# Sixteen row loads from SyncE's queue to ScalarE's and a new order of the words after chunk 2's casts, in a chunked retention that feeds a GELU MLP

## The chip, the core and the metric

The kernel runs on one core of a Trainium2 chip. The metric is device time in microseconds of one launch. Five compute engines take part: TensorE (PE; its weight loads are shown as PEld), VectorE (DVE), ScalarE (ACT), GpSimd (POOL) and SyncE (SP), which here only issues DMAs. DMAs issued by SyncE, ScalarE and GpSimd stand in three queues (SPq, ACTq, POOLq). Each engine runs its instructions in the order of the program; between engines there are semaphores.

## The reference, cut to what matters

```python
B, H, S, D = 4, 8, 768, 64
gamma = 1.0 - 2.0 ** (-5.0 - np.arange(H))
state = np.zeros((B, H, D, D))
for t in range(S):
    state = gamma * state + einsum('bhd,bhe->bhde', k[:, :, t], v[:, :, t])
    y[:, :, t] = (1 / sqrt(D)) * einsum('bhd,bhde->bhe', q[:, :, t], state)
x = y.transpose(0, 2, 1, 3).reshape(B * S, H * D)      # 3072 x 512
h = x @ w_in                                           # 512 x 2048
g = 0.5 * h * (1.0 + np.tanh(c * (h + 0.044715 * h**3)))
out = g @ w_out                                        # 2048 x 512
```

Everything is float32 outside. Inside, the products take float16 operands and add up in float32.

## The kernel before

**Tiling.** The 768 tokens are cut into six chunks c = 0 to 5 of 128, with four batches b each; a chunk is thus 512 rows of the MLP. For each chunk and batch the rows of q, k and v are loaded as float32 tiles of 128 tokens by 512 (`L`, L308, tile r, 256 KB each, thirteen buffers), and cast or scaled to float16 (`PREP`: q and k give the tile qk, v from chunk 2 on is scaled by a constant). q and k are transposed: in chunks 0 and 1 by TensorE with a copy (`T`, `ET`), in chunks 2 to 5 by a transposing DMA on SyncE's queue (`DT`, L345). `A` makes the scores of a chunk on TensorE, `EA` scales them with the mask on VectorE, `YP` and `YI` make the output of a chunk from the state and from the scores, `EP` writes it to the tile x on VectorE with a decay. `SS` and `ES` (L430, four VectorE instructions) bring the state to the next chunk.

**The MLP.** Both products go by a Winograd form: seven products of half size in place of eight. It wants sums of blocks: of w_in (`WI`), of w_out (`WO`), of x (`SX`, tile sx, four a chunk) and of g (`SG`, tile sg, four for each chunk and each j). These sums are additions of two float16 tiles in SBUF of 128x512 and can stand on VectorE or on GpSimd. j = 0 to 3 numbers the quarters of the 2048 hidden columns. `M1:c,j,n` is product n of the first matrix product: four matmuls of 128x256 into one of three PSUM banks X, Y, Z of its (c, j). `CP` copies a bank to a tile h, `D1` adds a bank to h on VectorE (L216), `G` takes the GELU on ScalarE (L442) and writes g. `M2:c,n,a,f` is a part, again of four matmuls, of product n of the second matrix product; `CO`, `D2` and `ST` copy, add and store its result. Part of chunk 0 is computed without that form (`HB`, `GB`, `O0`, `EO`, `ST0`). A product M1:c,j,1 needs the x of its chunk's batches 0 and 1, thus `EP:c,0,0` and `EP:c,0,1`; its bank must have been read by the last user, which for M1:2,3,1 in the new text is EP:2,1,1 and for M1:3,0,1 is EP:3,0,0. Where a product adds to a bank that a copy or an addition still reads, it waits too: M1:3,0,4 adds to the bank that D1:3,0,22 reads. M1:3,0,6 needs the sum SX:3,2.

**What sets the order.** The text `ORDER` (L17 to L135) holds 1125 words. Lines L656 to L661 take one word after another and emit its instructions, so each engine's and each queue's order is that of its words in this text. The letter in a word is its engine (`V` VectorE, `A` ScalarE, `P` GpSimd, `S` SyncE); the numbers behind `@` are the buffers that it takes; a buffer that comes again makes the new word wait for the last reader of the old contents. A word `L:v,4,0,S@10` loads the rows of v of chunk 4, batch 0, on SyncE's queue into buffer 10. `HOLD` is a DMA of a few bytes on SyncE's queue that reads a weight tile, so what stands behind it waits until that tile has been loaded. `LD` loads a constant, `LWI` and `LWO` (L262, L267) load the weights through GpSimd's queue.

```python
    for word in ORDER.split():
        word, _, at = word.partition("@")
        kind, _, args = word.partition(":")
        slots[:] = at.split(",") if at else []
        made[kind](*(int(x) if x.lstrip("-").isdigit() else x for x in args.split(",") if x))
```

Two lines are shared by many kinds: L216 is every two-operand elementwise instruction (`EA`, `EP`, `SX`, `SG`, `WI`, `WO`, `D1`, `D2`, scaled casts), L219 every matmul. Copies and casts are L211 on ScalarE and L213 on the others.

## Time and profile before

| what | value |
|---|---|
| time, median of 3 runs (lowest to highest) | 200.77 us (200.41 to 201.9) |
| the profiled execution's own time | 200.09 us |
| its span, first to last instruction | 198.3 us |
| TensorE busy (share of the span), matmuls | 183.0 us (92%), 2111 |
| VectorE busy, instructions | 160.0 us (81%), 294 |
| GpSimd busy, instructions | 139.1 us (70%), 143 |
| ScalarE busy, instructions | 119.3 us (60%), 219 |
| mean granted clock of TensorE | 0.98 |
| DMA moved | 34.26 MB, mean 173 GB/s |

Times in the profile are microseconds from the start of the span; durations in the groups are a mean in ns. A line of the timeline has the start, the busy time, the engine, the line, the operation and its tiles (out<-in), how many in a row (x4) and, in brackets, how long the engine stood idle before it and what ended that. A start to the next start on the same engine is a step; two instructions in a row overlap a little, so that steps are shorter than single durations. The stretches list for each engine its busy time and its instructions between two moments. The table of the slices has one digit for each fortieth of the span, the busy share in tenths. The chain that ended last is followed back from the last instruction.

### The profile page before, as it was taken

What the parts mean: (1) busy time and instruction counts of PE and PEld (TensorE: products, weight loads), DVE (VectorE), ACT (ScalarE), POOL (GpSimd) and SP (SyncE); (2) the same over time, 40 slices, a digit from 0 to 9 for tenths busy, and PEclk for the clock granted to TensorE, in tenths of its full rate; (3) what the DMA queues carried; (4) which work ended last, traced back from release to release, by engine and by line L of the source; (5) the groups of instructions that cost most, each with busy time, mean ns of one, the idle gap of its engine ahead of it and who ended that gap; (6) DMA issues with size and microseconds to landing.
All of it is one profiled execution on the core that took longest, in us unless ns stands there. A gap on an engine that the chain in (4) does not pass through costs nothing.

```text
span 198.3 us, 5294 instructions
## 1 busy us (share of the span) xinstructions
PE 183.0 (92%) x2111; PEld 149.0 (75%) x2111; DVE 160.0 (81%) x294; ACT 119.3 (60%) x219; POOL 139.1 (70%) x143
## 2 busy tenths in 40 slices
...
DVE  0888979899678999998989999998897577674630
...
GB/s 144 288 239 243 203 334 234 295 239 333 270 195 235 214 211 258 213 212 216 244 226 190 209 178 155 53 150 27 94 0 0 86 23 58 106 0 56 141 201 136
DMA packets 80540, 34.26 MB, mean 173 GB/s; under 512 B 69060, under 2 KB 78404, under 8 KB 80516
## 3 DMA queue, kind: packets, MB, share of 16 engines
...
## 4 chain that ended last, share of the span: by engine, by line
PE 65%; DMA 19%; POOL 6%; DVE 4%; issue 2%; ACT 1%; ACTq 0%; SPq 0%; POOLq 0%; DVEq 0%
PE bank L219 65%; DMA w_in<-in_moe_w_in_dram 9%; DMA r<-in_q_dram 6%; DMA qkT<-qk 2%; DVE g L216 2%; DMA r<-in_v_dram 2%; POOL sx L216 2%; POOL t_out L216 1%; POOL qk L216 1%; POOL v L216 1%; DVE h L216 1%; DVE w_out L216 1%; POOL g L216 1%; POOL w_in L262 0%; POOL qk L213 0%
## 5 line engine op out<-in xcount | busy, mean ns | idle before, releaser
L219 PEld LDWEIGHTS <-g 128*128 128x128 f16 x624 | 60.4, 98 | 11.8 <-PE bank L338 0.3
L216 POOL TENSOR_TENSOR g<-g 128x512 f16<-128x512 f16 x46 | 54.5, 1204 | 17.9 <-DVE g L216 7.2
L219 PE MATMUL bank<-w_out,g 128*128 128x256 f16 (+1 forms) x384 | 60.4, 290 | 0.2 <-DMA w_out<-in_moe_w_out_dram 0.2
L216 DVE TENSOR_TENSOR h<-bank,h 128x512 f32<-128x512 f32 x69 | 46.0, 682 | 8.8 <-PE bank L219 4.4
L442 ACT ACTIVATE g<-h 128x512 f16<-128x512 f32 x69 | 42.7, 634 | 15.4 <-DVE h L216 15.0
L219 PEld LDWEIGHTS <-w_in 128*128 128x128 f16 x432 | 39.2, 98 | 6.2 <-issue 0.8
L211 ACT COPY h<-bank 128x512 f32<-128x512 f32 x57 | 32.7, 588 | 13.0 <-PE bank L219 12.6
L219 PEld LDWEIGHTS <-t_in 128*128 128x128 f16 x276 | 26.4, 98 | 9.9 <-issue 4.3
L219 PE MATMUL bank<-t_out,g 128*128 128x256 f16 x240 | 33.4, 273 | 0.0
L216 DVE TENSOR_TENSOR a<-bank,mask 128x512 f16<-128x512 f32 x48 | 30.0, 680 | 3.5 <-PE bank L219 3.4
L219 PE MATMUL bank<-x,w_in 128*128 128x256 f16 (+1 forms) x248 | 29.7, 259 | 0.4 <-DMA w_in<-in_moe_w_in_dram 0.2
L219 PE MATMUL bank<-sx,t_in 128*128 128x256 f16 x184 | 26.5, 273 | 2.3 <-ACT g L442 1.2
L219 PE MATMUL bank<-sx,w_in 128*128 128x256 f16 x184 | 26.7, 273 | 0.0
L216 DVE TENSOR_TENSOR g<-g 128x512 f16<-128x512 f16 x34 | 22.1, 669 | 3.1 <-ACT g L442 2.1
L442 ACT ACTIVATE g<-bank 128x512 f16<-128x512 f32 (+1 forms) x31 | 16.5, 549 | 8.4 <-PE bank L219 5.8
L211 ACT COPY o<-bank 128x512 f32<-128x512 f32 (+1 forms) x19 | 9.7, 516 | 18.2 <-PE bank L219 18.2
L216 POOL TENSOR_TENSOR v<-r,cst 128x512 f16<-128x512 f32 x16 | 16.9, 1061 | 4.0 <-DMA r<-in_v_dram 4.0
L216 DVE TENSOR_TENSOR o<-bank,o 128x512 f32<-128x512 f32 (+1 forms) x18 | 10.6, 595 | 8.9 <-PE bank L219 8.7
L211 ACT CAST qk<-r 128x512 f16<-128x512 f32 x20 | 12.1, 620 | 6.2 <-PE bank L219 2.2
L219 PE MATMUL bank<-x,t_in 128*128 128x256 f16 x92 | 13.8, 273 | 1.9 <-DVE h L216 1.9
L216 DVE TENSOR_TENSOR qk<-r,cst 128x512 f16<-128x512 f32 x13 | 9.2, 744 | 6.5 <-DMA cst<-rr_cst 4.1
L211 ACT COPY qkT<-bank 128x1024 f16<-128x1024 f16 x7 | 6.9, 1013 | 8.0 <-PE bank L338 8.0
...
## 6 DMA issues: line engine op xcount, KB each, us to landing
r<-in_v_dram SPq DMA_DIRECT2D x15, 256.0 KB, 4.8
r<-in_q_dram SPq DMA_DIRECT2D x15, 256.0 KB, 4.2
r<-in_k_dram SPq DMA_DIRECT2D x14, 256.0 KB, 4.6
out_dram<-o ACTq DMA_DIRECT2D x11, 256.0 KB, 3.8
r<-in_v_dram POOLq DMA_DIRECT2D x9, 256.0 KB, 8.3
out_dram<-o SPq DMA_DIRECT2D x9, 256.0 KB, 2.3
w_in<-in_moe_w_in_dram POOLq DMA_DIRECT2D x8, 256.0 KB, 9.6
r<-in_k_dram POOLq DMA_DIRECT2D x8, 256.0 KB, 8.6
```

The costliest lines, as they stand in the source:

```text
L211: nc.scalar.copy(out=out, in_=in_)
L216: EN[e].tensor_tensor(out=out, in0=in0, in1=in1, op=op)
L219: nc.tensor.matmul(out=out, lhsT=lhsT, rhs=rhs, start=start, stop=stop, skip_group_check=True)
L442: nc.scalar.activation(out=out, in_=in_, func=AF.Gelu_apprx_tanh, scale=1.0)
```

## The change

Both texts hold 1125 words and the same products, sums, copies and stores; what differs is order, engine and buffer. TensorE's first 79 words, VectorE's first 76, ScalarE's first 65, GpSimd's first 40 and the first 10 words of SyncE's queue have the same engine and order as before, with some buffers exchanged; this is about the first 52 us. Behind that point:

- Sixteen loads of rows go from SyncE's queue to ScalarE's. In ScalarE's order they are k,3,2 k,3,3 q,3,0 v,3,3 k,3,0 q,3,3 v,4,3 q,4,3 v,4,0 k,4,0 q,5,0 v,5,1 k,5,2 v,5,0 k,5,0 k,5,3. SyncE keeps 28 of its 44; GpSimd's 23 loads stay with it.
- 28 sums (three `SX`, the rest `SG`, `WO` and `WI`) go from GpSimd to VectorE, 21 go the other way. 17 copies (`CP`, `CO`) go from ScalarE to VectorE, 13 the other way. Eight casts go from ScalarE to GpSimd, six the other way. Six stores go from SyncE's queue to ScalarE's, four the other way. VectorE has 274 words where it had 263, ScalarE 248 for 236, GpSimd 130 for 135, SyncE 65 for 83.
- The words of all engines stand in a new order.

The stretch from chunk 2's transposes to D1:3,0,22, and the last words, in both texts:

```diff
--- before.py
+++ after.py
 ORDER = """
...
-DT:2,3@1 CP:1,1,22,V@0 WO:3,1,P D1:1,0,11 PREP:k,2,2,A@3 L:v,2,1,S@6 M1:1,0,6 O0:2,0@6 CP:1,3,12,V@3
-PREP:q,2,2,P PREP:v,2,2,P@0 M1:1,0,5@4 PREP:k,2,0,A@4 G:1,0,11@18 M1:1,3,7 M1:1,3,3 PREP:q,2,1,A CP:1,0,12,A@1
-WI:1,2,V O0:2,1 PREP:q,2,0,P DT:2,1@2 DT:2,2@3 D1:1,3,22 LD:S D1:1,3,12 M1:1,1,6 EO:1,A@1 DT:2,0@0 HOLD:1,3
-M1:1,1,3 L:v,3,3,S@1 WO:3,2,P G:1,3,22@19 CP:1,1,12,A@2 M1:1,0,7 WI:1,4,P G:1,3,12@20 M1:1,3,4 D1:1,1,12
-G:1,3,21@21 A:2,3@2,5 M1:1,1,7 M1:1,2,5@7 O0:2,2 M1:1,2,1@1 EA:2,3,1@0 CP:1,0,22,A@3 PREP:v,2,1,P@3 D1:1,0,22
-D1:1,1,22 WO:1,2,P G:1,1,12@22 G:1,1,22@23 EA:2,3,0 M1:1,0,3 L:k,3,0,S@2 M1:1,0,4 D1:1,0,12 O0:2,3
-CP:1,2,22,V@2 CP:1,2,11,A@0 L:k,3,2,S@8 L:v,3,0,S@3 G:1,0,21@24 M1:1,1,4 M1:1,2,6 L:q,3,3,S@11 A:2,1@5,2
-G:1,1,21@25 PREP:v,3,2,P@2 A:2,2@4,3 L:q,4,1,S@7 EO:2,V@2 EA:2,1,0@3 EA:2,2,1@1 G:1,0,22@26 A:2,0@0,6
-CP:1,2,12,A@3 G:1,0,12@27 PREP:v,2,0,P@1 WO:0,2,P EA:2,0,0@2 L:q,3,2,S@5 PREP:v,2,3,P@4 M1:1,2,3 O0:3,0@5
-O0:3,1 EA:2,0,1 L:q,3,0,S@4 M1:1,2,7 PREP:k,3,0,A@1 EA:2,1,1 YP:2,0@3,0 EA:2,2,0 L:k,3,3,S@0 L:k,5,1,S@6
-YP:2,1@6,2 D1:1,2,12 YI:2,0 SG:1,1,1,P@28 L:q,3,1,S@10 PREP:v,3,3,P@6 L:q,4,2,S@12 SG:1,3,1,P@29 YI:2,1 YI:2,2
-HOLD:0,0 YI:2,3 EP:2,0,1,V@0 SS:2,0@4 SS:2,3@7 D1:1,2,22 SS:2,2 EP:2,0,0,V SS:2,1 SG:1,1,2,P@30 ES:2,1,V
-PREP:k,3,2,A@4 L:k,3,1,S@9 O0:3,2 G:1,2,22@31 M1:1,2,4 M1:1,2,2@0 EP:2,1,1,V O0:3,3 M1:2,0,1@3 D1:1,2,11
-WO:0,3,P HOLD:0,3 WO:3,3,P ST0:2,S PREP:q,3,2,P L:v,3,1,S@2 PREP:q,3,3,A@0 M2:1,1,0,0@7 EP:2,1,0,V
-SG:1,1,4,V@32 M1:2,3,1@2 M2:1,2,0,0@0 EO:3,A@3 CP:2,0,11,A@1 M1:2,0,2@6 M1:2,3,2@5 SX:2,1,V@3 G:1,2,21@33
-G:1,2,12@34 M2:1,2,0,1 SG:1,0,3,V@35 G:1,2,11@36 PREP:q,3,0,A CP:2,3,11,A@2 M1:2,0,5@1 SX:2,2,V@2
-CP:2,0,22,A@3 L:k,4,0,S@1 M2:1,1,1,0 SG:1,0,1,V@37 ES:2,0,V M1:2,0,6 PREP:q,3,1,A@3 D1:2,3,11 M1:2,3,6
-SG:1,0,2,V@38 M2:1,1,1,1 SX:2,4,P@4 M2:1,5,0,0@4 CP:2,0,12,A@0 M1:2,0,3 M2:1,1,0,1 G:2,3,11@39 M2:1,2,1,0
-SX:2,3,V@0 CP:2,3,12,A@2 M2:1,5,1,0 M1:2,0,7 M1:2,3,7 L:q,5,3,S@8 SG:1,3,2,V@40 SG:1,2,1,V@0 DT:3,0@4
-D1:2,0,12 PREP:k,3,1,A SG:1,3,4,P@2 M2:1,5,0,1 SG:1,2,2,P@6 L:q,4,0,S@5 CO:1,11,A@4 D1:2,0,11 G:2,0,12@9
-D1:2,0,22 WO:2,3,P WO:1,3,V G:2,0,22@1 M1:2,3,5@5 CP:2,3,22,A@0 WO:2,4,P DT:3,2@5 M2:1,2,1,1 PREP:k,3,3,A
-M2:1,5,1,1 SG:1,0,4,V@3 PREP:q,4,2,A@2 D1:2,3,22 L:k,4,3,S@11 M1:2,1,5@1 G:2,0,11@13 L:v,4,2,S@4 M1:2,0,4
-D2:1,11, DT:3,3@6 M1:2,3,3 M1:2,3,4 DT:3,1@0 D1:2,3,12 M1:2,1,1@6 G:2,0,21@14 L:v,4,0,S@10 M1:2,1,2@0
-CP:2,1,22,V@3 CO:1,22,A@5 G:2,3,21@4 SG:1,2,4,P@5 CP:2,1,11,A@1 M2:1,6,1,0 M2:1,3,0,0 SG:1,2,3,V@7 M2:1,6,1,1
-M1:2,1,6 G:2,3,22@8 D1:2,1,11 PREP:v,3,1,P@5 G:2,3,12@11 A:3,0@5,3 A:3,2@2,0 PREP:v,3,0,P@7 L:k,4,1,S@9
-SG:2,0,3,P@12 SG:1,1,3,P@10 CP:2,1,12,A@0 M1:2,1,3 M2:1,3,0,1 M2:1,6,0,0 WO:3,4,V EA:3,2,0@2 M1:2,2,1@2
-M2:1,6,0,1 M2:1,3,1,0 M1:2,1,7 CO:1,12,A@2 M2:1,3,1,1 SG:1,3,3,P@15 EA:3,0,0@3 D1:2,1,12 EA:3,0,1 EA:3,2,1
-D1:2,1,22 A:3,3@5,1 A:3,1@3,0 M1:2,1,4 L:q,4,3,S@0 G:2,1,21@24 EA:3,3,0@1 EA:3,3,1 EA:3,1,1@0 EA:3,1,0
-L:v,5,2,S@12 CP:2,2,11,A@2 M2:1,7,1,0 M2:1,7,1,1 L:k,4,2,S@2 M2:1,7,0,0 PREP:v,4,0,P@1 D2:1,12, ST0:0,S
-YP:3,1@6,5 YP:3,0@1,0 YI:3,2 WO:0,4,P WO:1,4,P YI:3,3 SS:3,3@3 G:2,1,12@18 L:v,5,0,S@3 YI:3,0 G:2,1,22@22
-YI:3,1 EP:3,1,1,V@1 SS:3,1@4 G:2,1,11@28 EP:3,0,1,V SS:3,2 PREP:q,4,3,A@0 PREP:k,4,3,A SS:3,0 EP:3,0,0,V
-M2:1,7,0,1 D2:1,22, M1:2,2,5@5 PREP:k,4,2,P SG:2,1,1,P@37 EP:3,1,0,V M1:2,2,6 M1:2,2,2@0 M1:3,0,1@1
-CP:2,2,22,A@0 CP:2,2,12,A@3 CP:3,0,11,A@1 ES:3,1,V M2:1,4,1,0 M1:2,2,7 D1:2,2,22 M2:1,4,1,1 PREP:q,4,0,A@3
-PREP:k,4,0,P ES:3,0,V M2:1,4,0,0 PREP:v,4,2,P@4 SX:3,1,P@1 M1:2,2,3 SX:3,3,P@5 M1:3,1,1@6 D1:2,2,11
-L:q,5,1,S@10 L:q,5,0,S@0 M2:2,1,0,0@3 M1:3,0,2@4 DT:4,2@2 G:2,2,22@20 ST:1,12,S SX:3,2,P@3 M2:2,1,1,0
-M1:3,1,2@0 M2:1,4,0,1 PREP:k,5,1,P@4 PREP:q,5,1,P PREP:k,4,1,A@1 D1:3,0,11 CP:3,1,11,A@0 M2:2,2,0,0@4
-D1:2,2,12 M1:3,0,5@5 PREP:q,4,1,P G:2,2,11@0 M1:2,2,4 D1:3,1,11 CP:3,0,22,V@2 SX:3,4,V@2 SG:2,0,1,V@29
-SG:2,3,1,V@27 SG:2,3,2,P@34 M1:3,0,6 M2:2,1,0,1 G:3,0,11@33 G:2,2,12@36 SG:2,1,2,V@17 CO:1,21,A@0
-SG:2,0,2,P@25 G:2,2,21@30 SG:2,1,3,V@38 M2:2,2,0,1 M1:3,0,3 M1:3,1,6 L:v,4,3,S@11 CP:3,0,12,A@1 G:3,1,11@6
-L:k,5,0,S@2 CP:3,1,12,A@3 M1:3,1,5@0 A:4,2@7,2 SG:2,2,1,V@40 CP:3,1,22,A@0 DT:4,3@1 M2:2,2,1,0 D1:3,0,12
-EA:4,2,0@2 L:k,5,3,S@5 SG:2,0,4,P@3 M1:3,0,7 L:q,5,2,S@1 DT:4,0@3 D1:3,0,22 M2:2,2,1,1 M1:3,1,7 M2:2,1,1,1
...
-D2:5,22,0 ST:5,22,S,0 M2:5,4,1,0 D2:5,12,0 M2:5,4,0,0 ST:5,22,S,1 ST:5,12,S,0 CO:4,21,A@1 M2:5,4,1,1
-M2:5,4,0,1 M2:5,3,1,0 ST:4,21,A CO:5,21,A,1@4 M2:5,3,1,1 CO:5,21,A,0 D2:5,12,1 ST:5,21,A,0 ST:5,21,S,1
-ST:5,12,S,1
...
+DT:2,1@1 D1:1,0,22 D1:1,1,22 O0:2,3 D1:1,0,12 M1:1,2,1@0 G:1,1,12@22 DT:2,3@2 M1:1,1,4 SG:1,3,1,V@23 DT:2,2@3
+A:2,3@5,2 G:1,0,22@24 A:2,1@7,1 WO:1,2,P L:k,3,3,A@4 M1:1,0,4 CP:1,2,11,A@3 G:1,1,21@25 EA:2,3,1@0 G:1,1,22@26
+EO:2,A@2 DT:2,0@0 L:v,2,1,S@0 PREP:v,2,0,P@2 L:v,3,0,S@5 G:1,0,21@27 O0:3,0@6 LD:S M1:1,2,6 M1:1,2,5@2
+EA:2,1,0@3 A:2,2@3,4 EA:2,1,1 SG:1,3,2,V@28 SG:1,3,3,P@29 CP:1,2,12,A@2 SG:1,0,1,V@30 L:q,3,0,A@12 A:2,0@7,1
+WO:2,4,P PREP:v,3,2,P@1 CP:1,2,22,A@0 PREP:v,2,2,P@3 M1:1,2,7 EA:2,2,1@1 O0:3,1 EA:2,2,0 EA:2,0,0@2 EA:2,0,1
+WO:3,1,P M1:1,2,3 O0:3,2 L:q,3,1,S@1 EA:2,3,0 PREP:v,2,1,P@6 YP:2,0@4,3 YP:2,1@7,1 L:v,3,3,A@2 L:k,3,1,S@11
+D1:1,2,12 YI:2,0 SS:2,3@5 YI:2,2 YI:2,1 D1:1,2,22 EP:2,0,0,V@0 SG:1,0,3,P@31 SS:2,1@2 EP:2,0,1,V G:1,2,12@32
+G:1,2,22@33 SS:2,0 YI:2,3 PREP:k,3,2,A@3 SG:1,1,1,P@34 SS:2,2 L:q,3,2,S@3 O0:3,3 PREP:k,3,3,P@1 EP:2,1,1,V
+L:k,3,0,A@9 M1:1,2,2@4 M2:1,1,0,0@3 EO:3,A@3 D1:1,2,11 G:1,0,12@35 M1:2,3,1@1 L:k,5,1,S@7 EP:2,1,0,V M1:1,2,4
+L:v,3,1,S@6 CP:2,3,11,A@2 L:q,3,3,A@10 PREP:v,3,0,P@5 PREP:q,3,0,A@2 M2:1,1,1,0 ES:2,0,V L:q,4,1,S@0
+SX:2,1,V@3 WO:3,2,V M1:2,0,1@6 M2:1,5,0,0@4 ES:2,1,V PREP:q,3,1,P@4 M1:2,3,2@7 G:1,2,11@36 CP:2,0,11,A@0
+M2:1,2,0,0@2 M2:1,2,1,0 SX:2,3,P@2 SX:2,2,P@0 M2:1,1,1,1 M2:1,2,1,1 M2:1,1,0,1 L:q,4,2,S@8 SG:1,0,2,V@37
+SX:2,4,P@4 WO:1,3,V M1:2,0,6 D1:2,3,11 G:1,2,21@38 ST0:0,S M2:1,5,1,0 SG:1,0,4,P@39 M1:2,0,2@5 PREP:k,3,1,A
+CO:1,11,V@4 L:k,4,2,S@4 M1:2,3,5@7 M1:2,3,6 PREP:k,3,0,A DT:3,0@4 CP:2,0,12,V@1 M1:2,0,7 M1:2,0,5@0
+SG:1,2,1,V@40 M2:1,5,1,1 D1:2,0,11 PREP:q,3,2,A G:2,3,11@0 CP:2,3,12,A@3 SG:1,2,2,V@2 DT:3,2@5 PREP:q,3,3,A
+M2:1,2,0,1 SG:1,1,2,V@6 M1:2,3,7 DT:3,1@6 G:2,0,11@9 CP:2,0,22,A@2 CP:2,3,22,A@0 L:v,4,3,A@5 SG:1,1,3,V@1
+WO:0,3,V L:q,4,3,A@12 M2:1,5,0,1 DT:3,3@0 M1:2,1,2@5 D2:1,11, M1:2,3,3 D1:2,3,22 M1:2,1,1@2 D1:2,0,22
+M2:1,6,1,0 G:2,3,22@3 D1:2,3,12 M2:1,6,0,0 M1:2,0,3 SG:1,2,4,P@13 CP:2,1,11,A@0 L:q,4,0,S@1 SG:1,1,4,P@14
+D1:2,1,11 M1:2,0,4 CO:1,22,A@5 D1:2,0,12 M1:2,3,4 G:2,3,12@4 L:k,4,1,S@11 M1:2,1,6 G:2,0,21@5 A:3,2@7,5
+SG:1,3,4,P@21 A:3,0@0,6 G:2,3,21@7 M2:1,3,1,0 SG:1,2,3,V@8 EA:3,2,0@2 PREP:v,3,1,P@4 CP:2,1,12,A@3 M1:2,1,5@1
+M2:1,6,0,1 G:2,0,22@11 EA:3,0,1@1 M1:2,1,7 M2:1,6,1,1 L:v,4,0,A@9 EA:3,2,1 M2:1,3,0,0 EA:3,0,0 WO:1,4,P
+PREP:v,4,3,P@7 PREP:v,3,3,P@6 CP:2,1,22,A@2 WO:3,3,P G:2,1,11@12 WO:3,4,P A:3,1@7,6 D1:2,1,22 A:3,3@5,0
+EA:3,1,0@3 M1:2,1,3 M1:2,1,4 M1:2,2,1@7 M2:1,3,1,1 G:2,1,21@27 EA:3,3,0@0 EA:3,1,1 EA:3,3,1 M2:1,3,0,1
+PREP:k,5,1,P@0 L:v,4,2,S@3 YP:3,0@2,5 L:k,4,3,S@10 CO:1,12,A@0 L:q,5,1,S@6 YP:3,1@6,0 YI:3,2 D2:1,12,
+D1:2,1,12 YI:3,3 YI:3,0 YI:3,1 SS:3,0@4 SS:3,3@1 SS:3,2 CP:2,2,11,A@0 EP:3,1,0,V@1 SS:3,1 WO:2,3,P EP:3,0,0,V
+M1:2,2,6 G:2,1,22@10 L:v,5,2,S@5 EP:3,1,1,V M2:1,7,0,0 M2:1,7,1,0 M2:1,7,1,1 L:v,4,1,S@2 M1:2,2,5@6 EP:3,0,1,V
+PREP:q,4,2,P@2 M2:1,7,0,1 G:2,1,12@15 SX:3,1,V@5 CP:2,2,12,A@2 HOLD:0,0 PREP:q,4,3,A@1 M1:2,2,7 WO:0,4,V
+SG:2,3,1,P@16 G:2,0,12@18 PREP:k,4,2,P L:k,4,0,A@7 CP:2,2,22,A@3 M1:3,0,1@2 SG:2,0,1,P@30 D2:1,22, SX:3,2,P@1
+M1:3,0,2@0 ES:3,0,V M1:2,2,2@5 SG:2,3,2,V@35 CP:3,0,11,A@1 M2:1,4,1,0 ST:1,11,A D1:2,2,11 PREP:q,5,1,P
+D1:3,0,11 M1:2,2,3 M2:1,4,0,0 L:q,5,0,A@8 D1:2,2,12 M1:3,0,6 ES:3,1,V L:q,5,3,S@12 PREP:q,4,0,P@3 PREP:k,4,3,A
+M2:1,4,1,1 M2:2,1,0,0@4 M1:3,0,5@5 G:2,2,11@34 SX:3,4,P@0 M2:2,1,1,0 DT:4,2@1 CP:3,0,22,V@0 M1:3,1,1@0
+ST:1,12,A M1:3,1,2@6 PREP:k,4,0,A DT:5,1@2 G:2,2,12@17 SX:3,3,P@3 PREP:v,4,0,P@2 D1:2,2,22 M2:2,1,0,1
+G:3,0,11@25 CP:3,1,11,A@2 M2:1,4,0,1 M2:2,2,0,0@1 CO:1,21,V@4 SG:2,3,4,V@23 M2:2,1,1,1 SG:2,0,2,V@40
+G:2,2,22@37 PREP:q,4,1,A@4 SG:2,1,1,P@32 CP:3,0,12,A@1 D1:3,1,11 DT:4,0@3 L:v,5,1,A@4 M1:3,1,6 PREP:k,4,1,A
+M1:2,2,4 M1:3,0,3 M1:3,0,7 CP:3,1,12,V@3 G:2,2,21@6 SG:2,1,2,P@22 DT:4,3@4 D1:3,0,22 SG:2,1,3,P@19 M2:2,2,0,1
...
+M2:5,3,0,1 CO:4,21,V@0 M2:5,4,1,0 D2:5,12,0 M2:5,4,1,1 ST:3,21,A D2:5,11,1 M2:5,7,0,1 CO:5,21,V,1@3 ST:4,21,A
+M2:5,3,1,0 M2:5,3,1,1 D2:5,22,0 ST:4,12,S M2:5,4,0,0 D2:5,12,1 ST:5,21,A,1 ST:5,11,S,1 ST:5,12,A,0 ST:5,22,S,0
+M2:5,4,0,1 CO:5,21,A,0 ST:5,22,S,1 ST:5,12,S,1 ST:5,21,A,0
 """
...
+    def WLI(j, kc, e):
+
+        t = new("r32", ("wi32", j, kc), [128, 512], F32)
+        for u in range(2):
+            row = u * 256 + kc * 64
+            EN[e].dma_start(
+                out=t[u * 64:(u + 1) * 64], in_=moe_w_in[row:row + 64, j * 512:(j + 1) * 512]
+            )
+
+    def WLO(j, kc, e):
+        t = new("r32", ("wo32", j, kc), [128, d_model], F32)
+        fc = 4 * j + kc
+        EN[e].dma_start(out=t, in_=moe_w_out[fc * 128:(fc + 1) * 128])
+
+    def CWLI(j, kc, e):
+        copy_on(e, w_in[j][:, kc], tiles["wi32", j, kc])
+
+    def CWLO(j, kc, e):
+        copy_on(e, w_out[j][:, kc], tiles["wo32", j, kc])
...
```

`WLI`, `WLO`, `CWLI` and `CWLO` are defined and entered in the table of kinds, and no word of the new text uses them. VectorE's words from D2:1,12 to D1:3,0,22 are, before and after:

```text
before  D2:1,12 EP:3,1,1 EP:3,0,1 EP:3,0,0 D2:1,22 EP:3,1,0 ES:3,1 D1:2,2,22 ES:3,0 D1:2,2,11
        D1:3,0,11 D1:2,2,12 D1:3,1,11 CP:3,0,22 SX:3,4 SG:2,0,1 SG:2,3,1 SG:2,1,2 SG:2,1,3
        SG:2,2,1 D1:3,0,12 EA:4,2,0 D1:3,0,22
after   D2:1,12 D1:2,1,12 EP:3,1,0 EP:3,0,0 EP:3,1,1 EP:3,0,1 SX:3,1 WO:0,4 D2:1,22 ES:3,0
        SG:2,3,2 D1:2,2,11 D1:3,0,11 D1:2,2,12 ES:3,1 CP:3,0,22 D1:2,2,22 CO:1,21 SG:2,3,4
        SG:2,0,2 D1:3,1,11 CP:3,1,12 D1:3,0,22
```

157 lines of the change are left out of this document (81 added, 76 removed).

## The prediction

> **What bounds the kernel now.** I read the table of engines first, then the slices, then TensorE's idle time by stretch, and last the instructions at which that idle time ends.
>
> ```profile
> span 198.3 us, 5294 instructions
> PE 183.0 (92%) x2111; PEld 149.0 (75%) x2111; DVE 160.0 (81%) x294; ACT 119.3 (60%) x219; POOL 139.1 (70%) x143
> ...
> DVE  0888979899678999998989999998897577674630
> ...
> PE 65%; DMA 19%; POOL 6%; DVE 4%; issue 2%; ACT 1%; ACTq 0%; SPq 0%; POOLq 0%; DVEq 0%
> ```
>
> TensorE is busy 183.0 of 198.3 us and heads the chain that ended last. What a new order can win is its idle time alone, and VectorE, at nine tenths in most slices up to the 27th, is second. The next view gives busy time by stretch; its columns are PE, PEld, DVE, ACT, POOL, then the granted clock, the share of the DMA engines and GB/s.
>
> ```profile
> 52.00:72.00 20.00, 20.00 (x251) 14.32 (x249) 17.37 (x31) 12.93 (x24) 19.90 (x21) 1.00 0.95 214
> 72.00:84.00 12.00, 11.71 (x108) 10.36 (x106) 11.55 (x23) 10.86 (x23) 9.27 (x9) 1.00 1.08 232
> 84.00:93.00 9.00, 8.53 (x117) 6.74 (x118) 8.68 (x14) 3.83 (x9) 4.96 (x5) 1.00 0.96 204
> 93.00:112.00 19.00, 16.93 (x228) 14.70 (x217) 17.64 (x32) 12.37 (x24) 17.02 (x18) 1.00 1.06 218
> 112.00:130.00 18.00, 18.00 (x256) 15.56 (x255) 17.54 (x35) 14.11 (x27) 12.93 (x13) 1.00 0.67 134
> 130.00:165.00 35.00, 35.00 (x390) 30.46 (x388) 28.98 (x47) 20.39 (x38) 26.37 (x25) 1.00 0.18 54
> 165.00:194.00 29.00, 29.00 (x268) 26.00 (x266) 16.22 (x31) 9.93 (x21) 11.85 (x10) 1.00 0.29 101
> ```
>
> The two orders part at about 52 us. From there to 194 us TensorE idles 0 + 0.29 + 0.47 + 2.07 = 2.83 us and is full afterwards. So the change can win at most 2.83 us, 1.4%. In the last row 268 matmuls of 256 columns take 29.00 us, 0.108 us each; a word M1 or M2 (four of them) costs TensorE 0.433 us, and no word of it is added or removed. Two rows hold the big stall, three what led to it:
>
> ```profile
> 92.27 1.04 POOL L216 TENSOR_TENSOR v<-r,cst 128x512 f16<-128x512 f32 x1 [4.04 <-DMA r<-in_v_dram]
> ...
> 103.66 0.60 PE L219 MATMUL bank<-sx,t_in 128*128 128x256 f16 x4 [0.42 <-POOL sx L216]
> ...
> 104.36 4.50 DVE L216 TENSOR_TENSOR g<-g 128x512 f16<-128x512 f16 x5
> ...
> 110.71 0.60 PE L219 MATMUL bank<-x,t_in 128*128 128x256 f16 x4 [1.65 <-DVE h L216]
> ...
> 88.83 0.56 SPq L308 DMA_DIRECT2D r<-in_v_dram  x1
> ```
>
> GpSimd waits 4.04 us for rows of v (PREP v,4,0) that SyncE issued only at 88.83. Its sums of x then come late (0.42 us at M1:3,0,6). VectorE spends 4.50 us on five sums of g and only then does D1:3,0,22, on which M1:3,0,4 waits 1.65 us. SyncE was late because its queue runs in order and transposes stand in it:
>
> ```profile
> 64.31 3.92 SPq L308 DMA_DIRECT2D r<-in_q_dram  x4
> 68.34 3.21 SPq L308 DMA_DIRECT2D r<-in_k_dram  x2
> ...
> 85.00 3.78 SPq L345 DMA_TRANSPOSE qkT<-qk  x2
> ```
>
> **The change part by part.** Arithmetic and products are the same words; a comparison of the two lists by engine gives what follows.
>
> (1) *Sixteen row loads go from SyncE to ScalarE.* SyncE has 28 loads where it had 44, 10 instead of 16 between chunk 2's last transpose and chunk 3's first. All four transposes of chunk 3 then follow without a load between them, and L:v,4,0 no longer stands behind them. I count the 4.04 us wait on GpSimd as gone, and with it what came of it. What is late next is VectorE, in (2). The gain is bounded by 0 and 2.83; I book all 2.83 as removed and price the new waits apart.
>
> The cost is ScalarE's. An issue holds its engine:
>
> ```profile
> 0.74 0.49 ACTq L308 DMA_DIRECT2D r<-in_k_dram  x1
> 5.26 2.67 ACTq L308 DMA_DIRECT2D r<-in_q_dram  x1
> 113.09 0.39 ACTq L648 DMA_DIRECT2D out_dram<-o  x1
> ...
> L308 SPq DMA_DIRECT2D r<-in_q_dram x15: 394/917/2661, 5.0 to 106.1; - x15
> ```
>
> No row shows ScalarE issuing a load between 52 and 112 us. Its own issues bound it by 0.39 and 2.67; I take 0.8, near SyncE's median 0.917 for rows of q, and a little less since ScalarE's loads stand further apart. Thirteen of the sixteen lie before chunk 4's first half is done, 13 x 0.8 = 10.4 us. ScalarE idles 20 - 12.93 + 12 - 10.86 + 9 - 3.83 + 19 - 12.37 = 20.0 us of those 60 and the change takes four copies and two casts from it besides, so the idle time covers the issues in total. Not everywhere: CP and G stand behind them, D1 on VectorE waits for CP, TensorE for D1. I take 0.5 us for that, bounds 0 and 4 (rival 2). Each such load also waits for the cast that frees its row buffer. By the order, those casts stand some 2 to 10 us of TensorE work ahead of the load, so I put nothing for it. Two casts on ScalarE, k,4,0 and k,5,3, read rows that it issued itself 5 to 6 us of TensorE work earlier, against this landing time (last number, us):
>
> ```profile
> r<-in_k_dram SPq DMA_DIRECT2D x14, 256.0 KB, 4.6
> ```
>
> Were a landing 2 us later, the copies behind that cast would be 1 us late; it lies within the bounds above.
>
> The Trainium skill, page "DMA: Bandwidth & Descriptors", section "Issuing engines are not separate DMA queues", speaks against this part: DMAs from any engine run on the same 16 DMA engines, so a second issuing engine saves issue time only. The trace agrees so far that one queue of rows beside GpSimd's fills them (shares 0.95 to 1.08 until 112 us). By that rule the rows land no sooner in total; that is rival 3.
>
> (2) *Sums move between GpSimd and VectorE.* VectorE gains 28 words from GpSimd and gives 21; it gains 17 copies from ScalarE and gives 13: 11 words more, some 7 x 0.6 + 4 x 0.6 = 6.6 us on 160. VectorE's prices:
>
> ```profile
> 62.60 3.68 DVE L216 TENSOR_TENSOR a<-bank,mask 128x512 f16<-128x512 f32 x6 [0.51 <-PE bank L219]
> ...
> L430 DVE SCALAR_TENSOR_TENSOR st<-st,cst,bank 128x128 f16<-128x128 f16 x32 | 8.9, 338 | 0.0
> L216 DVE TENSOR_TENSOR sx<-sx,x 128x512 f16<-128x512 f16 x2 | 0.8, 414 | 0.0
> ```
>
> Six in a row from PSUM take 3.68, 0.60 a step. ES is four of the second row, 1.04 a step. A sum of two operands in SBUF takes 0.41 alone and 4.50/5 = 0.90 beside a busy GpSimd. Three stretches count, with these rows of the timeline:
>
> ```profile
> 52.07 1.03 PE L219 MATMUL bank<-w_out,g 128*128 128x512 f16 x4
> 52.93 0.60 PE L219 MATMUL bank<-sx,t_in 128*128 128x256 f16 x4
> ...
> 54.01 1.29 DVE L216 TENSOR_TENSOR h<-bank,h 128x512 f32<-128x512 f32 x2 [0.55 <-PE bank L219]
> 56.41 0.69 DVE L216 TENSOR_TENSOR h<-bank,h 128x512 f32<-128x512 f32 x1 [1.12 <-ACT h L211]
> ...
> 70.94 0.68 DVE L216 TENSOR_TENSOR x<-bank,dec 128x512 f16<-128x512 f32 x1
> ...
> 92.59 0.68 DVE L216 TENSOR_TENSOR o<-bank,o 128x512 f32<-128x512 f32 x1
> ...
> 93.84 0.62 PE L219 MATMUL bank<-a,v 128*64 128x128 f16 x16
> 94.29 0.54 PE L219 MATMUL bank<-v,qk 128*64 128x64 f16 x24
> ...
> 109.98 0.67 DVE L216 TENSOR_TENSOR h<-bank,h 128x512 f32<-128x512 f32 x1
> ```
>
> *To chunk 2's x.* Before: 21 words of 0.60 and one ES, 13.6 us, no SBUF sum, between 56.4 and 71.6 us. After: 20 words of 0.60 and five SBUF sums (two weight sums, three of g), 12.0 + 5 x 0.41 to 0.90 = 14.1 to 16.5 us. VectorE is free from 55.3 us and would be through EP:2,1,1 (two steps before the end) at 68.2 to 70.6 us, if it never waited. TensorE without a stall reaches the user of that word, M1:2,3,1, after 18 words M1 or M2 (0.433), 7 O0 (52.07 to 52.93, 0.86) and 14 small ones (93.84 to 94.29 holds two, 0.23 each; 3.4 with two double ones and four shorter): 7.8 + 6.0 + 3.4 = 17.2 us after 52.9, at 70.1. VectorE is late by 0 to 0.5, and if it waits 2.63 us as in the first row of stretches, by 0.7 to 3.1. I take 0.9, near the middle of these and nearer the cheap end, since a sum can fill a wait.
>
> *To chunk 3's x.* After: 25 words of 0.60, two ES and ten SBUF sums, 17.1 + 4.1 to 9.0 = 21.2 to 26.1 us; TensorE's way from M1:2,3,1 to M1:3,0,1 is 24.8 us by the same count. Slack 3.6 to lateness 1.3. Between 71 and 93 us the eight sums of g of before took 0.60 each,
>
> ```profile
> L216 DVE TENSOR_TENSOR g<-g 128x512 f16<-128x512 f16 x8 | 4.7, 602 | 0.0
> ```
>
> and at 0.60 it is 23.1. I take 0.3 for waits; bounds 0 and 1.3.
>
> *From D2:1,12 to D1:3,0,22.* 23 VectorE words in either order. Before: fifteen of 0.60, two ES, six SBUF sums, 9.0 + 2.1 + 0.8 + 4.5 = 16.4 us of work, from 92.6 to 110.65, 18.1 us. After: sixteen of 0.60, two ES, five SBUF sums, 9.6 + 2.1 + 4.5 = 16.2 us. TensorE's way from YP:3 to M1:3,0,4 is 31 x 0.433 + 2.4 for the small words = 15.8 us. So 0.4 is late at the least, and 1.8 with the 1.36 us that VectorE idled in the row 93 to 112. I take 0.9. The five sums of g in a row are gone, but copies and weight sums took their place: this stall shrinks, it doesn't vanish.
>
> The Trainium skill, page "SBUF — State Buffer", section "Who interferes with whom", says that a VectorE instruction with two SBUF inputs and a GpSimd instruction that reads SBUF exclude each other, the later blocking wholly. The trace shows 0.41 against 0.90, so blocking is partial on average; by the rule at its worst a sum would be 0.41 + 1.16, an estimate, and the first stretch 3 us later still.
>
> (3) *The rest of the order.* After 130 us VectorE has more than 6 us idle in 35 and TensorE none: nothing. Ahead of 52 us instructions and engines are the same, but some PSUM banks and row buffers are swapped; I take 0, bounds -0.2 and +0.2. At the end TensorE's last word is followed by a ScalarE copy in place of a VectorE addition:
>
> ```profile
> 193.91 0.37 ACT L211 COPY o<-bank 128x256 f32<-128x256 f32 x1
> ...
> 194.78 0.43 DVE L216 TENSOR_TENSOR o<-bank,o 128x256 f32<-128x256 f32 x1 [2.20 <-PE bank L219]
> ```
>
> 0.37 against 0.43: nothing.
>
> **Sum.** The profiled execution took 200.09 us, its span 198.3 and 1.8 around it. 200.09 - 2.83 + 0.5 + 0.9 + 0.3 + 0.9 = 199.86. The median of the three runs is 200.77, 0.68 above the profiled one; on that base the forecast is 200.5 us: one set of stalls traded for another.
>
> **Rivals.**
>
> *1. Faster.* The SBUF sums run at 0.41 to 0.64 and VectorE, never waiting, keeps up: 0.5 us of new stalls in all, 198.4. For it: GpSimd stood idle 2.7 us in 72 to 84 and 4.0 in 84 to 93, so sums there run alone. Against it: the last stretch is late by 0.4 even so.
>
> *2. Slower: the row issues hold ScalarE.* Place: ScalarE between 52 and 112 us. If the DMA engines are full, an issue waits for room as at 5.26 (2.67) or as SyncE's at 68.34 (3.21 for two). It decides from 20.0 / 13 = 1.5 us an issue: then ScalarE's idle time is used up and every copy of M1's banks comes late. At 1.8 us it is 23.4 - 20.0 = 3.4 us over, with the 0.6 of late casts 4.0: 204.5. For it: VectorE has no reserve in these stretches. Against it: ScalarE's loads stand one or two at a time between other words, and the single rows of SyncE at 88.83 (0.56) and the median 0.917 are far below 1.5.
>
> *3. The spreading does not do what it says.* The DMA engines are full, rows come no sooner, GpSimd waits again at some cast and 2.07 us instead of 0.9 are lost behind it: 201.7.
>
> **How the numbers follow.** Forecast 0.45 (own range 199.2 to 202.4), rival 1 0.19, rival 2 0.22, rival 3 0.14. Faster or slower by 1% (2.0 us) is about what a measurement of this kernel can tell from no change. Below 198.76 lie rival 1 and a little of the forecast, 0.20; above 202.78 rival 2 and the forecast's and rival 3's upper parts, 0.27; between, 0.53. The range is 198.3 to 204.4: the floor, 200.77 - 2.83 = 197.9, is nearly reached, and above it most of rival 2 is in.
>
> **What would show it.** Right: no wait of GpSimd for rows over 1 us between 84 and 112 us; TensorE's idle time after 52 us spread over 57 to 93 in small waits for VectorE, 2 to 3 us in all; VectorE at 9.5 of 10 there; ScalarE issues of 0.5 to 1 us. Wrong: issues on ScalarE of 1.5 us and more with waits for ACT h ahead of D1 (rival 2), TensorE idle below 1 us (rival 1), or one long wait of any engine for rows (rival 3). A wait that the counts by engine can't show, between two engines in a new order, would make it wrong without any of them.

## The result

| kernel | median | lowest to highest | ratio to before, 95% interval |
|---|---|---|---|
| before, measured beside the changed kernel | 200.99 us | 199.50 to 201.90 | |
| changed | 198.61 us | 198.32 to 199.05 | 0.990 [0.987, 0.993] |

The changed kernel is 1.0% faster by the ratio; the medians lie 2.4 us apart. A ratio leaves out runs that are over 1.5% above the fastest of their kernel, so it can differ a little from the quotient of two medians. Measured once more on another occasion it took 198.76 us, ratio 0.991 [0.988, 0.994]. The forecast was 200.5 us with a range of 198.3 to 204.4: the time lies in the range, 0.3 us above its floor, near the 198.4 us of the rival "faster", and outside the forecast's own range of 199.2 to 202.4. The profiled execution took 198.52 us (before 200.09).

### The profile page after: what moved, and what is told of

Read it like the earlier page. It is cut to its first block, busy times and chain, and to the rows that moved or that the text cites. A ratio compares the mean times of both kernels' runs of the same rounds, so it can differ in the third digit from the quotient of the medians.

```text
span 196.7 us, 5295 instructions
## 1 busy us (share of the span) xinstructions
PE 183.2 (93%) x2111; PEld 150.2 (76%) x2111; DVE 166.1 (84%) x305; ACT 116.4 (59%) x213; POOL 132.9 (68%) x138
## 5 line engine op out<-in xcount | busy, mean ns | idle before, releaser
L218 PEld LDWEIGHTS <-g 128*128 128x128 f16 x624 | 60.4, 98 | 12.0 <-PE bank L357 0.5
L215 POOL TENSOR_TENSOR g<-g 128x512 f16<-128x512 f16 x44 | 51.6, 1190 | 16.2 <-DVE g L215 12.0
L218 PE MATMUL bank<-w_out,g 128*128 128x256 f16 (+1 forms) x384 | 58.9, 291 | 0.4 <-DMA w_out<-in_moe_w_out_dram 0.4
L461 ACT ACTIVATE g<-h 128x512 f16<-128x512 f32 x69 | 42.2, 632 | 18.7 <-DVE h L215 14.3
L215 DVE TENSOR_TENSOR h<-bank,h 128x512 f32<-128x512 f32 x69 | 45.4, 682 | 8.7 <-PE bank L218 7.7
L218 PEld LDWEIGHTS <-w_in 128*128 128x128 f16 x432 | 39.3, 98 | 7.0 <-issue 1.3
L210 ACT COPY h<-bank 128x512 f32<-128x512 f32 x55 | 31.5, 588 | 13.4 <-PE bank L218 11.8
L218 PE MATMUL bank<-t_out,g 128*128 128x256 f16 x240 | 33.9, 273 | 0.0
L218 PEld LDWEIGHTS <-t_in 128*128 128x128 f16 x276 | 26.3, 98 | 7.1 <-issue 1.8
L215 DVE TENSOR_TENSOR a<-bank,mask 128x512 f16<-128x512 f32 x48 | 29.8, 680 | 2.0 <-PE bank L218 1.7
L218 PE MATMUL bank<-x,w_in 128*128 128x256 f16 (+1 forms) x248 | 30.2, 259 | 0.9 <-DVE o L215 0.9
L218 PE MATMUL bank<-sx,t_in 128*128 128x256 f16 x184 | 26.5, 273 | 1.9 <-POOL sx L215 1.2
L218 PE MATMUL bank<-sx,w_in 128*128 128x256 f16 x184 | 26.3, 273 | 0.0
L215 DVE TENSOR_TENSOR g<-g 128x512 f16<-128x512 f16 x36 | 23.6, 681 | 0.0
L461 ACT ACTIVATE g<-bank 128x512 f16<-128x512 f32 (+1 forms) x31 | 16.4, 553 | 11.2 <-PE bank L218 11.1
L210 ACT COPY o<-bank 128x512 f32<-128x512 f32 (+1 forms) x17 | 9.3, 547 | 20.3 <-PE bank L218 20.2
L215 POOL TENSOR_TENSOR v<-r,cst 128x512 f16<-128x512 f32 x16 | 17.4, 1096 | 0.0
L215 DVE TENSOR_TENSOR qk<-r,cst 128x512 f16<-128x512 f32 x13 | 9.2, 748 | 5.9 <-DMA cst<-rr_cst 4.0
L218 PE MATMUL bank<-x,t_in 128*128 128x256 f16 x92 | 13.7, 273 | 0.3 <-DVE h L215 0.3
L212 POOL CAST qk<-r 128x512 f16<-128x512 f32 x14 | 8.8, 636 | 6.7 <-DMA r<-in_k_dram 3.2
L215 POOL TENSOR_TENSOR sx<-x,sx 128x512 f16<-128x512 f16 x5 | 6.5, 1294 | 9.9 <-DVE sx L215 9.9
L215 DVE TENSOR_TENSOR o<-bank,o 128x512 f32<-128x512 f32 (+1 forms) x18 | 10.5, 595 | 2.2 <-PE bank L218 2.1
```

What stands on the lines that cost most here:

```text
L210: nc.scalar.copy(out=out, in_=in_)
L212: EN[e].tensor_copy(out=out, in_=in_)
L215: EN[e].tensor_tensor(out=out, in0=in0, in1=in1, op=op)
L218: nc.tensor.matmul(out=out, lhsT=lhsT, rhs=rhs, start=start, stop=stop, skip_group_check=True)
L461: nc.scalar.activation(out=out, in_=in_, func=AF.Gelu_apprx_tanh, scale=1.0)
```

## The profile after

In the changed kernel's file the lines are shifted: elementwise instructions are L215, matmuls L218, copies and casts L210 on ScalarE and L212 elsewhere, GELU L461, row loads L327. The table of engines and VectorE's slices:

```profile
span 196.7 us, 5295 instructions
PE 183.2 (93%) x2111; PEld 150.2 (76%) x2111; DVE 166.1 (84%) x305; ACT 116.4 (59%) x213; POOL 132.9 (68%) x138
...
DVE  0897989899699999999999989998998597768641
```

The span is 1.6 us shorter. VectorE is 6.1 us busier, as counted (some 6.6), GpSimd 6.2 us less. The same stretches as before (PE, PEld, DVE, ACT, POOL, clock, DMA share, GB/s):

```profile
52.00:72.00 20.00, 19.91 (x247) 14.22 (x246) 19.30 (x31) 12.36 (x24) 16.91 (x18) 1.00 1.12 248
72.00:84.00 12.00, 11.10 (x103) 9.79 (x101) 11.88 (x25) 8.00 (x16) 10.27 (x9) 1.00 1.08 224
84.00:93.00 9.00, 9.00 (x169) 7.52 (x169) 8.81 (x15) 6.28 (x13) 6.54 (x7) 1.00 1.07 241
93.00:112.00 19.00, 18.26 (x194) 15.72 (x189) 19.00 (x34) 13.08 (x24) 18.77 (x19) 1.00 0.98 209
130.00:165.00 35.00, 34.75 (x384) 30.54 (x382) 29.95 (x53) 18.18 (x33) 20.51 (x19) 1.00 0.17 55
```

Between 52 and 112 us TensorE idles 0.09 + 0.90 + 0 + 0.74 = 1.73 us where it idled 2.83, and 0.25 after 130. VectorE is busy 58.99 of these 60 us (before 55.23). The instructions at which the idle time ends:

```profile
81.97 0.60 PE L218 MATMUL bank<-x,w_in 128*128 128x256 f16 x4 [0.90 <-DVE o L215]
...
107.11 0.40 PE L218 MATMUL bank<-qkT 64*128 64x128 f16 x8 [0.49 <-DVE h L215]
...
108.31 0.60 PE L218 MATMUL bank<-x,t_in 128*128 128x256 f16 x4 [0.25 <-DVE h L215]
...
130.50 0.61 PE L218 MATMUL bank<-sx,t_in 128*128 128x256 f16 x4 [0.25 <-DVE h L215]
```

All four wait for VectorE: M1:2,1,1 for the bank of D2:1,11, A:4,2 for that of D1:3,1,11, M1:3,0,4 for D1:3,0,22, M1:4,0,5 for D1:4,0,11. TensorE's waits of before on GpSimd's sum of x and on chunk 3's transposes are gone, and so is GpSimd's wait for rows of v.

The 1.6 us of span come from four places. TensorE reaches M1:1,3,6 at 49.59 us (before 49.90): 0.31. Its idle time from 52 to 112 us is 1.10 less, that after 130 is 0.25 more. From the end of the last matmul to the end of the span it is 3.24 us (before 3.56): 0.32. Together 1.48.

## The experiments

Theory 1 was the prediction's first step: spreading the rows takes away GpSimd's wait for v, and with it the stall. Theory 2: the order of the words does it, VectorE's above all. Each ratio is to the kernel before, measured beside it.

**The rows alone, from both sides.** First the changed kernel with the sixteen loads back on SyncE:

```diff
-L:k,3,2,A@8  ...  L:v,4,0,A@9  ...  L:k,5,3,A@7
+L:k,3,2,S@8  ...  L:v,4,0,S@9  ...  L:k,5,3,S@7
```

> The changed kernel with its sixteen row loads back on SyncE's queue, at the same words; everything else as changed. Theory 1 (the rows): rows of v stand behind chunk 3's transposes again, GpSimd waits more than 1 us for rows between 84 and 112 us, TensorE's idle time between 93 and 112 us grows from 0.74 us (19 - 18.26) to 2 us or more, 200 to 201 us. Theory 2 (the order alone): TensorE's idle time there stays within 0.3 us of 0.74 and the time is 198.4 to 198.9 us.

198.73 us, ratio 0.993 [0.990, 0.996]: not to be told from the changed kernel. GpSimd's scaled casts of v between 84 and 112 us, in this kernel (busy, mean ns, then idle time before them), and its last stretch:

```profile
L215 POOL TENSOR_TENSOR v<-r,cst 128x512 f16<-128x512 f32 x5 | 5.4, 1081 | 0.0
...
93.00:112.00 19.00, 18.31 (x216) 15.96 (x212) 19.00 (x34) 12.80 (x23) 17.94 (x18) 1.00 1.14 241
```

No wait for rows, though all 44 loads that are not GpSimd's stand in one queue, and TensorE idles 0.69 us where the changed kernel idles 0.74. Nor did the rows of v,4,0 get much earlier: SyncE issues them at 87.23 us here and at 88.83 in the kernel before. It is their cast that moved, to 102.27 us in GpSimd's new order, where it stood at 92.27. The new order took the wait away, not the second queue. Theory 1 falls.

Then the kernel before with only these loads on ScalarE:

```diff
-L:k,3,0,S@2  ...  L:v,4,0,S@10  ...  L:k,5,3,S@5
+L:k,3,0,A@2  ...  L:v,4,0,A@10  ...  L:k,5,3,A@5
```

> The kernel before with only the sixteen row loads on ScalarE's queue, at their own words. Theory 1 (the rows): GpSimd's wait of 4.04 us for rows of v goes below 1 us, TensorE's waits of 0.42 us on the sum of x and of 1.65 us on D1:3,0,22 go with it, about 2 us less than before, 198.5 to 199 us. Theory 2 (the order): GpSimd's wait goes, but D1:3,0,22 still stands behind five sums of g on VectorE and M1:3,0,4 still waits 1 us or more, 199.8 to 200.8 us. If the issues hold ScalarE, it is slower than before.

200.91 us, ratio 1.004 [1.001, 1.007]: no gain, if anything a small loss. Its timeline shows why, first ScalarE, then TensorE:

```profile
69.19 0.37 ACTq L308 DMA_DIRECT2D r<-in_q_dram  x1
69.61 0.62 ACT L211 CAST qk<-r 128x512 f16<-128x512 f32 x1 [4.62 <-DMA r<-in_q_dram]
72.39 0.41 ACTq L308 DMA_DIRECT2D r<-in_k_dram  x1
72.89 0.62 ACT L211 CAST qk<-r 128x512 f16<-128x512 f32 x1 [2.67 <-POOL qk L213]
...
75.09 0.60 PE L219 MATMUL bank<-x,w_in 128*128 128x256 f16 x4 [1.63 <-ACT o L211]
```

The issues themselves take 0.37 and 0.41 us. But ScalarE computes nothing for 4.62 and 2.67 us up to the casts behind them, and 4.20 and 2.16 us of this pass before the loads L:q,3,0 and L:k,3,3 are issued; copies stand behind, and TensorE waits 1.63 us. It isn't their row buffers: the casts that read these last ended at 52.40 and 56.14 us. What the two loads wait for, by the program's list of semaphores:

```text
L308 DMACopy r_1234<-in_q_dram 128x8x64 [waits DMAHW3_49,DMAHW1_49]
L308 DMACopy r_1262<-in_k_dram 128x8x64 [waits DMAHW0_49,DMAHW6_49,DMASW1_49,Pool_49]
```

The first waits for earlier DMAs alone; eight such semaphores (DMAHW0 to 7) go round among the DMAs of both queues, so a load on ScalarE can wait for one of SyncE's to end. Counted in the order of the program, DMAHW3 tells the first load of the end of L:q,3,2 on SyncE's queue, and DMAHW6 tells the second of L:q,3,1. By the trace these landed at 69.12 and 72.29 us, 0.07 and 0.10 us before the two loads were issued. So the second load, too, stood behind a DMA, though the row of the cast behind it names GpSimd. By the start times of its words TensorE is 3.62 us behind the kernel before at M2:1,2,0,1 and 1.28 at M1:3,0,4. GpSimd's waits for v come to 0.8 us, and chunk 3's waits shrink as theory 1 said, but this doesn't pay for what is lost here. Theory 2 came within 0.1 us of the median; neither had the mechanism. The expectation's last sentence had the place, ScalarE, but it is held by what the loads wait for and not by the issues.

**VectorE's order.** In the kernel before, two words move behind D1:3,0,22:

```diff
-SG:2,2,1,V@40 ... D1:3,0,12 EA:4,2,0@2 ... D1:3,0,22
+D1:3,0,12 ... D1:3,0,22 EA:4,2,0@2 SG:2,2,1,V@40
```

> The kernel before with two of VectorE's words moved: SG:2,2,1 and EA:4,2,0 behind D1:3,0,22. Theory 2 (the order): M1:3,0,4 waits less than 0.3 us where it waited 1.65, the kernel is 1.3 to 1.6 us faster than before, 199.2 to 199.6 us. Theory 1 (the rows): VectorE's lateness comes from the rows of v and goes on behind M1:3,0,4, so the idle time turns up at M1:3,3,1 or A:4,3 instead and the time stays at 200.3 to 201 us.

199.32 us, ratio 0.993 [0.990, 0.996]. TensorE's rows (M1:3,0,6, M1:3,0,4 and M1:3,1,4):

```profile
104.06 0.60 PE L219 MATMUL bank<-sx,t_in 128*128 128x256 f16 x4 [1.19 <-POOL sx L216]
...
109.29 0.60 PE L219 MATMUL bank<-x,t_in 128*128 128x256 f16 x4
...
111.75 0.49 PE L219 MATMUL bank<-x,t_in 128*128 128x256 f16 x3 [0.55 <-DVE h L216]
```

M1:3,0,4 waits no more, as theory 2 said, and the time is where it put it. Part of the gain turns up again beside it, as theory 1 said: 1.19 us at M1:3,0,6 (before 0.42), where GpSimd was late again, and 0.55 at M1:3,1,4. The gain is 0.8 us by the median measured beside it (200.15) and 1.3 us by the ratio, so two words make a third to two thirds of what the whole change brought. GpSimd still waits for rows here, longer than before (4.04 and 1.42 us there):

```profile
91.51 1.04 POOL L216 TENSOR_TENSOR v<-r,cst 128x512 f16<-128x512 f32 x1 [3.66 <-DMA r<-in_v_dram]
97.39 0.61 POOL L213 CAST qk<-r 128x512 f16<-128x512 f32 x1 [2.60 <-DMA r<-in_k_dram]
```

So the 1.65 us at M1:3,0,4 came from VectorE's order and not from the rows, while the wait on the sum of x grew with GpSimd's lateness.

In the changed kernel three words move:

```diff
-SG:1,1,3,V@1 WO:0,3,V ... D2:1,11, ... D1:2,3,22 D1:2,0,22 D1:2,3,12 D1:2,1,11 D1:2,0,12
+D2:1,11, ... D1:2,3,22 D1:2,0,22 SG:1,1,3,V@1 D1:2,3,12 D1:2,1,11 WO:0,3,V D1:2,0,12
-SG:2,3,4,V@23 SG:2,0,2,V@40 D1:3,1,11
+D1:3,1,11 SG:2,3,4,V@23 SG:2,0,2,V@40
```

> The changed kernel with three of VectorE's words moved: SG:1,1,3 and WO:0,3 behind D2:1,11 (after D1:2,0,22 and D1:2,1,11), and D1:3,1,11 ahead of SG:2,3,4 and SG:2,0,2. Theory 2 (what is left of TensorE's idle time is VectorE's order): M1:2,1,1 no longer waits 0.90 us on D2:1,11 and A:4,2 no longer 0.49 us on D1:3,1,11, 1.0 to 1.4 us less than the changed kernel, 197.2 to 197.7 us. Rival (VectorE is full there, so the wait moves to the next word): within 0.3 us of the changed kernel's 198.6.

197.87 us, ratio 0.988 [0.984, 0.991], 0.2 us above what theory 2 expected. The wait on D2:1,11 is gone; a new one, at A:3,0, stands 4 us on (first TensorE, then VectorE):

```profile
85.84 0.40 PE L218 MATMUL bank<-qkT 64*128 64x128 f16 x8 [0.99 <-DVE h L215]
...
84.01 1.17 DVE L215 TENSOR_TENSOR w_out<-w_out 128x512 f16<-128x512 f16 x1
85.11 0.68 DVE L215 TENSOR_TENSOR h<-bank,h 128x512 f32<-128x512 f32 x1
```

A:3,0 takes the bank that D1:2,0,12 reads, and the weight sum that was moved stands right in front of it. So the rival "the wait moves on" holds for this word. It holds only as long as the sum stands ahead of a word that TensorE wants soon, which the next kernel tests by moving WO:0,3 one word further and three more sums:

```diff
-SG:1,0,1,V@30 EA:2,2,1@1 ... EA:2,0,1
+EA:2,2,1@1 ... EA:2,0,1 SG:1,0,1,V@30
-WO:0,3,V ... D2:1,11,  ...  D1:2,1,11 ... D1:2,0,12
+D2:1,11,  ...  D1:2,1,11 ... D1:2,0,12 WO:0,3,V
-SG:2,0,2,V@40 ... D1:3,0,22
+D1:3,0,22 SG:2,0,2,V@40
-SG:3,3,1,V@35 ... D1:4,0,11
+D1:4,0,11 SG:3,3,1,V@35
```

> The changed kernel with six of VectorE's words moved: SG:1,0,1 behind EA:2,0,1; SG:1,1,3 behind D1:2,0,22; WO:0,3 behind D1:2,0,12; D1:3,1,11 ahead of SG:2,3,4 and SG:2,0,2 behind D1:3,0,22; SG:3,3,1 behind D1:4,0,11. In the first such order the wait of 0.9 us on D2:1,11 went and one of 0.99 us on D1:2,0,12 came, as WO:0,3 stood ahead of it. Theory 2 (VectorE's order, word by word): that wait, and those at YI:2,0 (0.26), M1:3,0,4 (0.39) and M1:4,0,5 (0.43) go too, 1.5 to 2.1 us less idle time of TensorE than in the first order, 196.0 to 196.6 us. Rival (VectorE is full from 52 to 112 us, so a sum put behind one word is in front of the next): 197.6 to 198.2 us.

197.03 us, ratio 0.983 [0.978, 0.987]; the changed kernel measured beside it took 198.76 us. So six words bring 1.7 us, and TensorE has almost no idle time left:

```profile
52.00:72.00 20.00, 20.00 (x251) 14.48 (x249) 18.93 (x32) 12.70 (x24) 17.19 (x18) 1.00 1.14 244
72.00:84.00 12.00, 12.00 (x122) 10.61 (x121) 11.12 (x24) 9.46 (x19) 10.27 (x10) 1.00 1.11 243
84.00:93.00 9.00, 8.62 (x170) 7.16 (x165) 9.00 (x15) 4.91 (x10) 6.68 (x7) 1.00 0.99 223
93.00:112.00 19.00, 18.84 (x192) 16.02 (x190) 18.91 (x35) 13.65 (x25) 18.92 (x19) 1.00 0.96 209
```

It idles 0.54 us between 52 and 112 us where the changed kernel idles 1.73. The time is 0.4 us above what theory 2 expected. The rows were then put back on SyncE in this kernel, with the letters as in the first experiment:

> The changed kernel with the six words of VectorE moved (197.03 us), and with the sixteen row loads back on SyncE's queue. In the changed kernel the spreading showed no gain (198.73 against 198.76 us). If that holds with less idle time of TensorE to hide it: 196.7 to 197.4 us. If the rows were late only behind VectorE's words: waits of A on chunk 3's transposes and of GpSimd on rows over 1 us, 197.6 to 199 us.

196.86 us, ratio 0.986 [0.981, 0.991], the lowest median of all and not to be told from the one with the rows spread. With less idle time of TensorE to hide it, spreading still brings nothing. Yet the waits that the second expectation named are there: TensorE waits 0.14 and 0.28 us for chunk 3's transposes at A:3,2 and A:3,3, and GpSimd 1.91 us for rows:

```profile
85.99 2.05 POOL L215 TENSOR_TENSOR v<-r,cst 128x512 f16<-128x512 f32 x2 [1.91 <-DMA r<-in_v_dram]
```

With the rows spread these waits are missing. But TensorE then idles as much between 52 and 112 us, 0.54 us against 0.49 here: at A:3,3 the kernel with the rows spread is 0.87 us ahead, and at M1:3,0,1, 8 us on, 0.13. So spreading takes waits away, and TensorE waits elsewhere instead.

**Sums and copies.** The 49 sums go back to their former engines in the new order (28 times V to P, four of them sums of x, 21 times P to V):

```diff
-SG:1,3,1,V@23  ...  SX:2,2,P@0  ...
+SG:1,3,1,P@23  ...  SX:2,2,V@0  ...
```

> The changed kernel with the 49 sums that changed engine (28 on VectorE, 21 on GpSimd) back on their former engines, at the same words. By the prediction's step 2 VectorE is relieved of seven sums net, some 0.4 to 0.9 us each, and the waits on VectorE between 52 and 112 us get smaller: 197.8 to 198.3 us. Rival (GpSimd's sums, 1.2 us each, become late in an order made for other engines): waits on GpSimd's sums of g and x at M2 and M1, 1 to 4 us slower, 199.6 to 202.6 us.

202.22 us, ratio 1.009 [1.006, 1.012]. The rival is right about the size, though its waits are mostly VectorE's. By the start times of its words TensorE falls behind the second profile of the changed kernel by 0.98 us at M1:2,3,1, 1.45 at M2:1,4,1,0 and 3.01 at M1:3,1,4. Its longest wait, M1:3,3,2, and what VectorE did then:

```profile
112.79 0.60 PE L218 MATMUL bank<-x,w_in 128*128 128x256 f16 x4 [1.43 <-DVE a L215]
...
110.18 1.96 DVE L215 TENSOR_TENSOR g<-g 128x512 f16<-128x512 f16 x2
```

VectorE has fewer words, but two of its returned sums stand ahead of EA:4,2. The mirror image is the kernel before with the sums where the changed kernel has them:

> The kernel before with the 49 sums on the engines that the changed kernel has them on, at the words of before. If the sums' engines alone bring the gain (28 sums of 1.2 us off GpSimd for 0.4 to 0.9 us on VectorE): 198.5 to 199.8 us. If engine and order only work together, as the sums on their former engines in the new order suggest (3.5 us slower): 201.5 to 204 us, with TensorE waiting on VectorE's h.

205.09 us, ratio 1.025 [1.019, 1.031]. The profiled execution was the fastest, 203.34 us. In it M1:3,0,4 waits 2.52 us (before 1.65), with VectorE first held by GpSimd:

```profile
112.23 0.60 PE L219 MATMUL bank<-x,t_in 128*128 128x256 f16 x4 [2.52 <-DVE h L216]
...
107.73 2.65 DVE L216 TENSOR_TENSOR g<-g 128x512 f16<-128x512 f16 x2 [2.90 <-POOL g L216]
```

One and the same exchange costs 3.5 us undone in the new order and over 4 us done in the old one. What an engine is worth for a sum depends on the words around it.

The copies that changed engine, put back in the new order (`CP` and `CO`, 17 times V to A, 12 times A to V; EO:2, the thirteenth word that went to ScalarE, stays there):

> The changed kernel with the copies (CP, CO) that changed engine back: 17 from VectorE to ScalarE, 12 from ScalarE to VectorE, at the same words. By the prediction's step 2 VectorE, which is full between 52 and 112 us, gains three words of 0.6 us net there, and ScalarE, busy 12.4 of 20 us and less, has room: 198.0 to 198.5 us. Rival (as with the sums, the order is made for the engines that the words are on): a copy on ScalarE stands behind a GELU that waits, M1's banks come free late, 199.5 to 202 us.

200.32 us, ratio 1.003 [1.000, 1.006]: 1.6 us slower than the changed kernel. But not where step 2 looked. Between 52 and 112 us TensorE falls up to 0.7 us behind and catches up again: at M1:3,0,4 it is 0.2 us ahead of the second profile of the changed kernel, at M1:4,0,5 0.5. It loses 0.77 us from M1:4,0,5 to M1:4,3,3, where it waits for a copy that has gone back to VectorE,

```profile
145.19 0.60 PE L218 MATMUL bank<-sx,w_in 128*128 128x256 f16 x4 [0.62 <-DVE h L212]
```

and 0.6 more by M1:5,3,5; the time from the last matmul to the end grows from 3.24 to 3.95 us. The casts, the stores and the buffers that changed were not changed alone in any run.

**The end and the spread of before.** The kernel before with the last products in another order:

```diff
-M2:5,4,0,0 ... M2:5,4,1,1 M2:5,4,0,1 M2:5,3,1,0 ... M2:5,3,1,1 CO:5,21,A,0 D2:5,12,1
+M2:5,3,1,0 M2:5,3,1,1 D2:5,12,1 M2:5,4,0,0 ... M2:5,4,1,1 M2:5,4,0,1 ... CO:5,21,A,0
```

> The kernel before with TensorE's last words in the order of the changed kernel: M2:5,3,1,0 and M2:5,3,1,1 ahead of M2:5,4,0,0, with D2:5,12,1 behind them, so that the last word is followed by the copy CO:5,21,A,0 and a store on ScalarE's queue. The time from the end of the last matmul to the end of the span was 3.56 us before and 3.2 us in the changed kernel. If the order of the last words makes that difference: 3.1 to 3.3 us here. If it is the time a store takes to land, which no order sets: 3.5 us or more. Either is too little for the medians to tell.

200.64 us, ratio 1.003 [0.999, 1.007], and the time behind the last matmul is 4.19 us, longer than before. The first expectation fails. The last two products end close together here, and both copies of them stand behind each other on ScalarE:

```profile
194.50 0.81 ACT L211 COPY o<-bank 128x256 f32<-128x256 f32 x2 [3.34 <-PE bank L219]
```

In the changed kernel the first of the two is an earlier copy on VectorE. But that isn't the difference: the store behind the last copy is issued 0.44 us after the last matmul in both kernels. What differs is the time from that issue to the end, 3.75 us here and 2.81 in the changed kernel:

```profile
195.34 0.36 ACTq L648 DMA_DIRECT2D out_dram<-o  x1
...
193.94 0.34 ACTq L667 DMA_DIRECT2D out_dram<-o  x1
```

So the second expectation is right in size and place: it is the time that the last store takes to land. Whether no order sets it, as it says, is open. In this kernel SyncE issues two more stores in the 0.44 us before it (at 194.90 and 195.32 us), in the changed kernel its last one is issued at 193.18. That the stores delay each other is likely, and was not tried alone.

Last, a second profile of the kernel before:

> The kernel before once more, for a second profile. Its times run from 197.9 to 201.9 us. If the spread comes from the time at which rows land, TensorE's idle time at M1:3,0,6 and M1:3,0,4 (0.58 and 1.82 us lost in the first profile) differs by some tenths to 1.5 us, and everything ahead of 84 us agrees within 0.3 us; if it comes from the start, the two profiles differ ahead of 20 us.

199.19 us, 0.9 less than the first. GpSimd's wait for v and TensorE's two waits at chunk 3 are:

```profile
90.77 1.04 POOL L216 TENSOR_TENSOR v<-r,cst 128x512 f16<-128x512 f32 x1 [2.64 <-DMA r<-in_v_dram]
...
102.75 0.60 PE L219 MATMUL bank<-sx,t_in 128*128 128x256 f16 x4 [0.43 <-POOL sx L216]
109.80 0.60 PE L219 MATMUL bank<-x,t_in 128*128 128x256 f16 x4 [1.65 <-DVE h L216]
```

The wait for v is 1.4 us shorter, and the next one, for rows of k, 0.6 us longer (2.03 for 1.42). GpSimd's sums of x come 0.9 us earlier, TensorE does too, and so its two waits are what they were (0.42, 1.65). What differs is chunk 3's A. In the first profile two of them wait for transposes, here none does; of the second wait the row is:

```profile
90.50 0.40 PE L219 MATMUL bank<-qkT 64*128 64x128 f16 x8 [0.34 <-DMA qkT<-qk]
```

By the start times of its words TensorE loses 0.29 us at A:3,2 and 0.51 at A:3,1 against the second profile, 0.80 of the 0.91 us that it is behind at M1:3,0,6. So most of the difference between the two is when these transposes are issued and land (SyncE issues them 1.0 to 1.3 us earlier here); the expectation looked for it in the rows and at another place. In the changed kernel no A waits for a transpose in either profile, and its times lie within 1.0 us instead of 2.4 and more.

## Why the prediction was right, and where it was wrong

The time lies in the range, and that is partly luck. The direction was left open with most weight, 0.53, on "within 1%"; 198.61 us lies 0.15 below that bound, in the part that was given 0.20. The range reached so far down for the sake of rival 1, whose reason does not hold (see (2)). The forecast itself is 1.9 us too high, and the terms account for it:

- **What goes: right in size.** The five stalls of before were booked as gone, 2.83 us. They are, but for 0.25 us at M1:3,0,4. For the largest, 1.65 us, a run shows why: two of VectorE's words. For the other four, which part of the new order removes them was not tried.
- **(1) The sixteen rows: the step that failed.** The wait of GpSimd was to go because SyncE has fewer loads. It goes with these loads on SyncE too, as the cast of v stands 10 us later in the new order. "And with it what came of it" is wrong for the larger part: with GpSimd's waits for rows even longer, 3.66 and 2.60 us, the 1.65 us at M1:3,0,4 went when two of VectorE's words moved. Only the 0.42 us on the sum of x followed GpSimd. The wait for v and the long stall were neighbours, and the first was no measure of the second.
- **(1) ScalarE's issues: overpriced, and the wrong thing priced.** 0.8 us an issue was taken; the rows of the changed kernel give (minimum, median, maximum in ns)

```profile
L327 ACTq DMA_DIRECT2D r<-in_k_dram x9: 374/375/769, 0.7 to 119.8; - x9
L327 ACTq DMA_DIRECT2D r<-in_q_dram x7: 374/459/2667, 1.3 to 97.6; - x7
L327 ACTq DMA_DIRECT2D r<-in_v_dram x5: 374/387/1391, 63.3 to 114.0; - x5
```

  and no wait of TensorE for ScalarE is among those left: 0 instead of 0.5. Rival 2, 204.5 us, was wrong by its price of 1.8 us an issue. What can hold ScalarE is what a load waits for. The step looked at the casts that free the row buffers and put nothing; in the old order loads waited for other DMAs instead, and TensorE was 3.6 us late.
- **(2) VectorE, three stretches: 0.9 + 0.3 + 0.9 = 2.1 forecast, 0.09 + 0.90 + 0.74 = 1.73 measured.** All three waits are for VectorE, as said; the first was overpriced, the second was three times its price. There D2:1,11 stood behind three sums of g (2.04 us) and a weight sum (1.37), which a count of VectorE's work from chunk to chunk cannot show. The sums' price was right on average:

```profile
L215 DVE TENSOR_TENSOR g<-g 128x512 f16<-128x512 f16 x12 | 10.0, 858 | 0.0
```

  0.86 us against the 0.90 and 0.41 to 0.90 used. By stretch it was not: the five, ten and five sums of the three stretches, weight sums with them, took 1.05, 0.67 and 1.10 us in the mean. VectorE never waited for long in the first, and came through EP:2,1,1 at 70.30 us, as counted (68.2 to 70.6). So rival 1 came near the time for a reason that does not hold: the sums do not run at 0.41 to 0.64, VectorE is full (58.99 of 60 us), and TensorE still idles more than the 0.5 us it allowed.
- **(2) What the exchange of the sums is worth was left out.** Sums given to VectorE were booked as a cost alone. With the exchange undone in the new order the kernel is 3.5 us slower.
- **(3) The rest: 0 forecast.** 0.32 us at the end and 0.31 ahead of 52 us were gained, 0.25 lost after 130. At the end the step compared a copy with an addition; the difference lies behind the issue of the last store. The 0.31 is no effect shown: over all kernels here, of either order, M1:1,3,6 starts between 49.43 and 49.90.
- **The base.** The 0.68 us between before's profile and its median were added; the changed kernel's median is 0.09 above its own. The spread of before belongs to its order: the times of every kernel in the old order spread over 1.8 us or more, those of every kernel in the new one over 1.1 or less.

New waits 0.6 us below forecast, head and end 0.6, base 0.6: together 1.8 of the 1.9 us.

Of the signs named ahead, two came: no wait of GpSimd for rows over 1 us between 84 and 112 us, and VectorE busy 9.8 of 10. Two did not: TensorE's waits come to 2.0 us, but in one of 0.90 and three behind 93 us instead of small ones spread over 57 to 93, and ScalarE's issues take 0.4 us instead of 0.5 to 1.

The Trainium skill's "DMA: Bandwidth & Descriptors", section "Issuing engines are not separate DMA queues", was cited against the sixteen loads on ScalarE: a second issuing engine saves issue time only. Both pairs of runs agree: 198.73 us with one queue against 198.76 with the rows spread, and 196.86 against 197.03. Rival 3 drew from it that GpSimd's wait would come back; in the changed kernel it did not, with the rows on either queue. The Trainium skill's rule in "SBUF — State Buffer", section "Who interferes with whom", at its worst would have made each sum 1.57 us, an estimate from that page; the mean of 0.86 lies between that and the 0.41 alone, as in the kernel before, and the dearest took 1.37.
